# Transposing the 32 left-over columns of x before or after the split into high and low parts

## The chip, the cores and the metric

The kernel runs on one core of a Trainium2 chip. The metric is the device time of one execution in microseconds (us); the time before is the median of three runs.

## The reference

```python
x = A_x                                   # 1 x 2048 x 576
xn = _layernorm(x, axis=-1)
return x + _A_ref(xn, A_w_r, A_w_i) + _B_ref(xn, B_w_gate, B_w_up, B_w_down)

def _A_ref(x, w_r, w_i):                  # spectral filter
    X = jnp.fft.rfft2(x, axes=(-2, -1)) * (w_r + 1j * w_i)
    return jnp.fft.irfft2(X, s=(S, D), axes=(-2, -1))

def _B_ref(x, w_gate, w_up, w_down):      # gated linear unit, 576 -> 4608 -> 576
    h = _sigmoid(x @ w_gate) * (x @ w_up)
    return h @ w_down
```

All inputs are float32. S = 2048 rows, D = 576 columns, F = 4608 hidden columns.

## The kernel before

Every large product runs on TensorE in F32R, a reduced form of float32. To keep the accuracy, each operand is split into a high part (rounded to F32R by a ScalarE copy) and a low part (VectorE subtracts the high part from the original), and three products are added: high x high, low x high, high x low.

The gated unit is the main load. The 2048 rows are handled as two pairs of chunks of 512 rows (`p` = 0, 1). In each pair the 576 columns are halved (288 each), and most products use a seven-product scheme on 2 x 2 blocks: A11, A12, A21, A22 and the sums S1 to S4 of such blocks. For each of the 36 hidden tiles, `unit` (or `plain` for the first two tiles) runs products (`prod`, L648) of 512-wide matmuls; the down projection (`down`, L755) and later the "seven" rounds (L846) and the spectral stages (`phase1b`, `phase2`, `phase3`) are threaded between them by generators that are advanced once in each product (`beside`, `turn`).

The products need x with columns on the partitions, so each block of the normalized x is transposed on TensorE. A block is 128 rows x 288 columns: two tiles of 128 columns and 32 left-over columns (`REM`). The tile `X` holds, for each block and each of its 512 rows, five slices: the high parts of the two 128-column tiles (slices 0 and 1), the left-over slice (2), and the two low parts (3 and 4). The left-over slice has 96 used partitions (`KR` = 3 x 32): the 32 columns' high part twice and their low part once; the weights stand against it as high, low, high, so that one matmul does all three products. `STEPS` puts it last of the seven matmuls of a product.

The functions around the change, with the names that the views show:

- `prep` normalizes a row tile into `xa` (L409) and then splits its left-over columns into `rma`: `rem_hi` writes the high part twice with one ScalarE copy (L391), `rem_lo` the low part with one VectorE subtraction (L396). `sums` forms the sums of blocks (L421 to L424) and splits the left-over columns of the results into `rma` and `rm34` (shown as `rm`).
- `fill` brings one block for two row tiles into `X`. It takes a pair of PSUM banks (`px`, from a pool of two pairs that the down projection and the spectral stages use too), does four transposes of 128 x 128 against the F32 identity `idf` (L438) and two of the split 96 columns against the F32R identity `idr` (L439), copies the results into `X` on ScalarE (L442 for the wide tiles, L443 for the left-over slice), and subtracts on VectorE for the low parts (L444).

There are 32 fills: in each of the two pairs, two for each of A11, A12, A21, A22 and S1 to S4. The first four come at the start of the kernel, ahead of the first product; twelve more fall within the first part of the first pair, and sixteen at the change to the second pair, all among products.

At the start a list of matmuls on the identity (`todo`, L904) keeps TensorE occupied; some use all 128 rows, some the halves `H0` and `H1`. Four more (L922) stand between the first fills.

A scheduler places each instruction on its engine at build time, by estimated times; `placed` and `keep_in_program_order` hold some of them to the written order.

Of the kernel before, what the change touches and what calls it, by code (L numbers as in the profile page):

```python
# [10 lines left out]
F32R = mybir.dt.float32r  # L11
I32 = mybir.dt.int32
AF = mybir.ActivationFunctionType
OP = mybir.AluOpType
PSUM = bass.MemoryType.PSUM

P = 128
# [9 lines left out]
TPC = CW // P  # L27
PAIRS = S // (2 * CW)
TPP = 2 * TPC
KT = 2  # L30
REM = HD - KT * P
# [6 lines left out]
KR = 3 * REM  # L38
# [94 lines left out]
def spectral_glu_kernel(ctx: ExitStack, tc: tile.TileContext, x, w_r, w_i, w_gate, w_up, w_down, out):  # L133
    nc = tc.nc
    con = {k: nc.inline_tensor(v, name=f"c_{k}").ap() for k, v in _constants().items()}

    def f32(ap):
        return ap.bitcast(F32)
# [6 lines left out]
    def pair(name):  # L145
        return ps.tile([P, 2, 512], F32, tag="pp", name=name, bufs=2)

    fix = ctx.enter_context(tc.tile_pool(name="fix", bufs=1))
    idf = fix.tile([P, P], F32, name="idf")
    idr = fix.tile([P, P], F32R, name="idr")  # L150
# [49 lines left out]
    R = {}  # L200
# [23 lines left out]
    def placed(ins):  # L224
        if late_input[0]:
            tc.keep_in_program_order(ins)
# [121 lines left out]
    def moments(src, t, pool):  # L348
        st = pool.tile([P, 2, 6], F32, tag="st", name=f"st{t}", bufs=2)
        for i in range(2):  # L350
            placed(nc.vector.bn_stats(st[:, i, :], src[:, i * HD:(i + 1) * HD]))
        nc.vector.bn_aggr(mv[:, t, :], st.rearrange("p a b -> p (a b)"))

    def scales(t0, n, pool, table):
        ts = slice(t0, t0 + n)
        rs = pool.tile([P, 4, n], F32, tag="rs", name=f"rs{t0}", bufs=2)
        ve, r0, w0, w1 = (rs[:, i] for i in range(4))
        nc.vector.tensor_scalar(ve, mv[:, ts, 1], EPS, None, op0=OP.add)
        if table:
            nc.scalar.activation(w0, ve, AF.Sqrt)  # L360
            nc.vector.reciprocal(r0, w0)
            steps = 1
        else:

            nc.vector.tensor_scalar(w1.bitcast(I32), ve.bitcast(I32), 1, None, op0=OP.logical_shift_right)
            nc.vector.tensor_scalar(r0.bitcast(I32), w1.bitcast(I32), -1.0, float(0x5F3759DF), op0=OP.mult, op1=OP.add)
            steps = 3
        nc.vector.tensor_scalar(ve, ve, -0.5, None, op0=OP.mult)
        for k in range(steps):
            nc.vector.tensor_tensor(w0, r0, r0, op=OP.mult)  # L370
            nc.vector.tensor_tensor(w0, w0, ve, op=OP.mult)
            o = rstd[:, ts] if k == steps - 1 else r0
            nc.vector.scalar_tensor_tensor(o, w0, 1.5, r0, op0=OP.add, op1=OP.mult)
        nc.vector.scalar_tensor_tensor(nmr[:, ts], mv[:, ts, 0], -1.0, rstd[:, ts], op0=OP.mult, op1=OP.mult)
# [5 lines left out]

    XS, XR, RM = {}, {}, {}

    def new_xs(p, m):
        XS[m] = R["pool"].tile([P, 5, HD], F32, tag="xa", name=f"xa{p}_{m}", bufs=TPC)

    def rem_hi(p, m, i, tag, bufs):
        rem = XS[m][:, i:i + 2, KT * P:]
        rm = R["pool"].tile([P, 2, 3, REM], F32R, tag=tag, name=f"{tag}{p}_{m}_{i}", bufs=bufs)  # L390
        nc.scalar.activation(rm[:, :, :2], rem.unsqueeze(2).to_broadcast([P, 2, 2, REM]), AF.Copy)  # L391
        RM[m, i] = rm

    def rem_lo(m, i):
        rm = RM[m, i]
        placed(nc.vector.tensor_tensor(rm[:, :, 2], XS[m][:, i:i + 2, KT * P:], f32(rm[:, :, 0]), op=OP.subtract))  # L396
        for k in range(2):
            XR[m, i + k] = rm[:, k].rearrange("p a b -> p (a b)")

    def rem_parts(p, m, i, tag, bufs):  # L400
        rem_hi(p, m, i, tag, bufs)
        rem_lo(m, i)

    def prep_hi(p, m, c):

        t = p * TPP + c * TPC + m
        b = XS[m][:, 2 * c:2 * c + 2]
        src = b if p else acc[t].rearrange("p (a d) -> p a d", a=2)
        nc.scalar.activation(b, src, AF.Identity, bias=nmr[:, t:t + 1], scale=rstd[:, t:t + 1])  # L409
        rem_hi(p, m, 2 * c, "rma", 2)  # L410

    def prep_lo(m, c):
        rem_lo(m, 2 * c)

    def prep(p, m, c):
        prep_hi(p, m, c)
        prep_lo(m, c)

    def sums(p, m):
        A11, A12, A21, A22, S1 = (XS[m][:, i] for i in range(5))  # L420
        nc.vector.tensor_tensor(S1, A21, A22, op=OP.add)  # L421
        nc.vector.tensor_tensor(A21, A11, A21, op=OP.subtract)
        nc.vector.tensor_tensor(A22, S1, A11, op=OP.subtract)
        nc.vector.tensor_tensor(A12, A12, A22, op=OP.subtract)  # L424
        rem_parts(p, m, 3, "rma", 2)
        rem_parts(p, m, 1, "rm34", TPC)

    XP = {"A11": 0, "A12": 1, "A21": 2, "A22": 3, "S4": 1, "S3": 2, "S2": 3, "S1": 4}

    def fill(p, k, mm):  # L430

        i, j0 = XA[k], XP[k]
        cols = slice(2 * mm * P, (2 * mm + 2) * P)
        pt = pair(f"px{p}_{k}_{mm}")
        for j in range(2):
            m = 2 * mm + j
            for q in range(KT):
                nc.tensor.transpose(pt[:, 0, (2 * q + j) * P:(2 * q + j + 1) * P], XS[m][:, j0, q * P:(q + 1) * P], idf)  # L438
            nc.tensor.transpose(pt[:KR, 1, j * P:(j + 1) * P].bitcast(F32R), XR[m, j0], idr)  # L439
        v = pt[:, 0].rearrange("p (q s) -> p q s", q=KT)  # L440
        o = X[:, i, :, cols]
        nc.scalar.activation(o[:, :KT], v, AF.Copy)  # L442
        nc.scalar.activation(o[:KR, KT], pt[:KR, 1, :2 * P], AF.Copy)  # L443
        nc.vector.tensor_tensor(o[:, KT + 1:], v, f32(o[:, :KT]), op=OP.subtract)  # L444

    def new_acc(p, m):
        t = p * TPP + m
        acc[t] = AC[:, m]
        load_x(acc[t], t)
# [460 lines left out]
        moments(acc[m], m, R["pool"])  # L910
    scales(0, 2, R["pool"], True)
    for m in (0, 1):
        prep_hi(0, m, 0)
    for m in (2, 3):
        moments(acc[m], m, R["pool"])
    for m in (0, 1):
        prep_lo(m, 0)
    scales(2, 2, R["pool"], True)
    for k in ("A11", "A12"):
        fill(0, k, 0)  # L920
    for n in range(4):
        tc.keep_in_program_order(nc.tensor.matmul(b0, idr, eye, start=False, stop=True, skip_group_check=True))  # L922
    for m in (2, 3):
        prep(0, m, 0)
    next(mk)
    next(mk)
    for k in ("A11", "A12"):
        fill(0, k, 1)
# [17 lines left out]
    def blocks(p, c):  # L946
        for mm in range(2):
            for m in (2 * mm, 2 * mm + 1):
                prep(p, m, c)
            for k in (1, 2):  # L950
                fill(p, f"A{c + 1}{k}", mm)
            yield
# [20 lines left out]
    def factors(p):  # L973

        for mm in range(2):
            for m in (2 * mm, 2 * mm + 1):
                sums(p, m)
                yield
            for k in ("S1", "S2"):
                fill(p, k, mm)  # L980
                yield
            if mm == 0:
                sides.append(late(p))
# [162 lines left out]
```

## Time and profile before

| | before |
|---|---|
| median of 3 runs | 1441.58 us (1441.42 to 1442.97) |
| profiled execution, span from first to last instruction | 1439.6 us |
| profiled execution, time of its own beside the span | not given by the page |
| TensorE matmuls busy | 1425.9 us (99%) |
| TensorE weight loads busy | 1254.3 us (87%) |
| VectorE busy | 1093.5 us (76%) |
| ScalarE busy | 652.3 us (45%) |
| mean granted TensorE clock | 0.996 |

In the profile PE is TensorE's matmuls, PEld its weight loads, DVE VectorE, ACT ScalarE, SP the queue that issues most transfers. A row such as `128*96 128x128` gives the rows and columns of the stationary operand and then the shape of the moving one. The busy time of a matmul runs from its start to its modelled end, and matmuls overlap; the chain of work that ended last shows instead how far each one moved the end.

### The profile page before, as it was taken

The page shows a single profiled execution, that of the slowest core. Times are in us where ns is not written, and L with a number is a line of the kernel's source. Part 1 is how long each engine was busy: PE and PEld are TensorE (multiplying, and loading weights), DVE is VectorE, ACT ScalarE, POOL GpSimd, SP SyncE. Part 2 cuts the span into 40 slices and gives each one's busy share as a digit, 9 for nine tenths or more (in the row PEclk, how much of TensorE's full clock was granted, in tenths as well). Part 3 has the DMA queues.
Part 4 walks back from the last instruction along what each step waited for, and adds up shares of the span by engine and source line. Part 5 has one row for each costly group of instructions (what it writes and reads, how often), then busy time and mean ns, then how long its engine had stood idle before and what let it go on. Part 6 is the DMA issues. An engine that isn't in the chain of part 4 may idle for free.

```text
span 1439.6 us, 21954 instructions
## 1 busy us (share of the span) xinstructions
PE 1425.9 (99%) x8073; PEld 1254.3 (87%) x8073; DVE 1093.5 (76%) x1798; ACT 652.3 (45%) x1122; POOL 4.8 (0%) x21
## 2 busy tenths in 40 slices
PE   8999999999999999999999999999999999999998
PEld 5888888888888888888888888888888889899997
DVE  6988788888888888756366787767888877766784
ACT  5644444444444444444345444444555534443432
POOL 0000000000000000000000000000000000000000
PEclk8999999999999999999999999999999999999999
DMA  6588788787777778664667767668998887776642
GB/s 209 207 277 294 263 295 285 254 274 258 263 261 255 262 254 277 230 231 167 226 210 203 212 197 214 196 198 275 271 275 272 267 276 246 228 224 198 204 126 83
DMA packets 184747, 338.86 MB, mean 235 GB/s; under 512 B 15808, under 2 KB 108480, under 8 KB 179776
## 3 DMA queue, kind: packets, MB, share of 16 engines
q1 hardware_dynamic: 183712, 336.15, 72.2%
q8 instruction: 64, 1.05, 0.3%
q10 hardware_dynamic: 928, 1.31, 0.3%
q14 instruction: 43, 0.35, 0.1%
HBM read 201.28 MB, written 136.12 MB: 234 GB/s over the span
## 4 chain that ended last, share of the span: by engine, by line
PE 94%; DVE 2%; DMA 1%; SPq 1%; ACT 1%; issue 1%; DVEq 0%; ACTq 0%
PE pB L648 23%; PE po L755 18%; PE pE L648 16%; PE pA L648 15%; PE ps L846 12%; PE pd L491 2%; PE pe L605 2%; PE pc L549 1%; PE py L576 1%; PE pa L503 1%; PE pb L532 1%; DMA raw<-in_B_w_up 1%; PE pf L475 1%; PE pz L588 1%; SPq L218 0%
## 5 line engine op out<-in xcount | busy, mean ns | idle before, releaser
L648 PE MATMUL pB<-X,w 128*128 128x512 f32 x1484 | 383.0, 395 | 1.9 <-ACT w L231 1.5
L648 PEld LDWEIGHTS pB<-X,w 128*128 128x128 f32 x1484 | 267.8, 188 | 51.8 <-ACT w L231 1.9
L648 PE MATMUL pE<-X,w 128*128 128x512 f32 x1064 | 272.5, 392 | 0.2 <-DVE y L713 0.2
L648 PE MATMUL pA<-X,w 128*128 128x512 f32 x1008 | 259.4, 395 | 0.3 <-DVE X L444 0.2
L648 PEld LDWEIGHTS pE<-X,w 128*128 128x128 f32 x1064 | 192.7, 188 | 34.6 <-DVE y L713 0.7
L648 PEld LDWEIGHTS pA<-X,w 128*128 128x128 f32 x1008 | 184.5, 190 | 33.9 <-DVE X L444 0.7
L755 PE MATMUL po<-wd,hh 128*128 128x288 f32 x1216 | 210.9, 295 | 0.0
L846 PE MATMUL ps<-wf,hs 128*128 128x288 f32 x1260 | 206.0, 296 | 0.3 <-issue 0.3
L846 PEld LDWEIGHTS ps<-wf,hs 128*128 128x128 f32 x1260 | 189.3, 188 | 19.4 <-DVE qs L856 1.9
L755 PEld LDWEIGHTS po<-wd,hh 128*128 128x128 f32 x1216 | 184.4, 188 | 11.2
L759 DVE TENSOR_TENSOR acc<-acc,po 128x576 f32<-128x576 f32 x168 | 126.0, 750 | 77.9 <-PE po L755 76.8
L231 ACT ACTIVATE w<-raw 128x768 fp32r<-128x768 f32 (+1 forms) x106 | 100.8, 952 | 115.6 <-PE pE L648 47.5
L755 PE MATMUL po<-wd,hl 128*128 128x288 f32 x608 | 128.9, 293 | 0.0
L856 DVE TENSOR_TENSOR qs<-qs,ps 128x576 f32<-128x576 f32 x112 | 84.1, 751 | 28.6 <-PE ps L846 27.9
L755 PEld LDWEIGHTS po<-wd,hl 128*128 128x128 f32 x608 | 98.7, 189 | 0.0
L733 DVE TENSOR_TENSOR y<-y,g 128x1024 f32<-128x1024 f32 x67 | 82.0, 1223 | 4.4 <-DVE y L732 0.5
L233 DVE TENSOR_TENSOR w<-raw,w 128x512 fp32r<-128x512 f32 (+1 forms) x106 | 82.0, 773 | 4.3 <-ACT w L231 3.3
L856 DVE TENSOR_TENSOR acc<-acc,ps 128x576 f32<-128x576 f32 x90 | 67.5, 750 | 22.9 <-PE ps L846 22.5
L716 ACT ACTIVATE g<-pB 128x512 f32<-128x512 f32 x68 | 40.7, 598 | 93.6 <-PE pB L648 93.5
L782 ACT ACTIVATE hs<-y 128x512 fp32r<-128x512 f32 x105 | 64.5, 628 | 34.3 <-DVE y L820 10.3
L732 DVE TENSOR_TENSOR y<-v,pE 128x512 f32<-128x512 f32 x67 | 45.9, 686 | 39.4 <-PE pE L648 39.3
L713 DVE TENSOR_TENSOR y<-v,pE 128x512 f32<-128x512 f32 x68 | 46.7, 687 | 33.7 <-ACT v L712 33.0
(166 smaller groups left out, 1678.8 us busy)
## 6 DMA issues: line engine op xcount, KB each, us to landing
w<-wsp SPq DMA_DIRECT2D x246, 320.0 KB
wsp<-w SPq DMA_DIRECT2D x34, 2240.0 KB
wdsp<-wd SPq DMA_DIRECT2D x36, 576.0 KB
wf<-tsp SPq DMA_DIRECT2D x60, 288.0 KB
wf<-wdsp SPq DMA_DIRECT2D x45, 288.0 KB
std<-in_B_w_down SPq DMA_DIRECT2D x36, 288.0 KB
raw<-in_B_w_gate SPq DMA_DIRECT2D x72, 128.0 KB
raw<-in_B_w_up SPq DMA_DIRECT2D x72, 128.0 KB
```

Of the source, the lines that this page charges most:

```text
L231: placed(nc.scalar.activation(o[:, :, :3, :], src, AF.Copy))
L233: placed(nc.vector.tensor_tensor(o[:, :, 3:, :], src[:, :, :KT, :], f32(o[:, :, :KT, :]), op=OP.subtract))
L648: nc.tensor.matmul(bank, w[:, sw, :], X[:, x, sx, :], start=start and j == 0, stop=stop and j == len(STEPS) - 1, skip_group_check=skip)
L713: nc.vector.tensor_tensor(y[:, 1], v[:, 1], bank["E"], op=OP.add)
L716: nc.scalar.activation(g[:, 1], bank["B"], AF.Sigmoid)
L732: nc.vector.tensor_tensor(y[:, 0], v[:, 0], bank["E"], op=OP.add)
L733: nc.vector.tensor_tensor(y, y, g, op=OP.mult)
L755: nc.tensor.matmul(pd[:, b, :HD], h[i], w[k][b], start=g == 0 and n == 0, stop=g == G - 1 and n == 2)
L759: nc.vector.tensor_tensor(a, a, pd[:, :, :HD], op=OP.add)
L782: nc.scalar.activation(hs[:, 0], src, AF.Copy)
L846: nc.tensor.matmul(pd[:, i, :HD], h[:, a, m], w[:, b], start=q == 0, stop=q == 2)
L856: nc.vector.tensor_tensor(o, o, pd[:, :, :HD], op=OP.add)
```

## The change

The left-over columns are no longer split before the transpose. `rem_hi`, `rem_lo`, `rem_parts`, `prep_hi` and `prep_lo` go, and with them the tiles `rma` and `rm34`. `fill` transposes the 32 columns as they are, in F32 against `idf`, into 32 partitions of PSUM. Behind the transpose ScalarE copies them twice (to partitions 0 to 31 and 32 to 63 of the left-over slice), and VectorE subtracts the first copy from the transposed columns and writes the low part to partitions 64 to 95.

```diff
-    def rem_hi(p, m, i, tag, bufs):
-        rem = XS[m][:, i:i + 2, KT * P:]
-        rm = R["pool"].tile([P, 2, 3, REM], F32R, tag=tag, name=f"{tag}{p}_{m}_{i}", bufs=bufs)
-        nc.scalar.activation(rm[:, :, :2], rem.unsqueeze(2).to_broadcast([P, 2, 2, REM]), AF.Copy)
-        RM[m, i] = rm
-
-    def rem_lo(m, i):
-        rm = RM[m, i]
-        placed(nc.vector.tensor_tensor(rm[:, :, 2], XS[m][:, i:i + 2, KT * P:], f32(rm[:, :, 0]), op=OP.subtract))
-        for k in range(2):
-            XR[m, i + k] = rm[:, k].rearrange("p a b -> p (a b)")
...
-    def prep_hi(p, m, c):
+    def prep(p, m, c):
...
         nc.scalar.activation(b, src, AF.Identity, bias=nmr[:, t:t + 1], scale=rstd[:, t:t + 1])
-        rem_hi(p, m, 2 * c, "rma", 2)
...
     def sums(p, m):
...
         nc.vector.tensor_tensor(A12, A12, A22, op=OP.subtract)
-        rem_parts(p, m, 3, "rma", 2)
-        rem_parts(p, m, 1, "rm34", TPC)
...
     def fill(p, k, mm):
...
-            nc.tensor.transpose(pt[:KR, 1, j * P:(j + 1) * P].bitcast(F32R), XR[m, j0], idr)
+            nc.tensor.transpose(pt[:REM, 1, j * P:(j + 1) * P], XS[m][:, j0, KT * P:], idf)
         v = pt[:, 0].rearrange("p (q s) -> p q s", q=KT)
         o = X[:, i, :, cols]
         nc.scalar.activation(o[:, :KT], v, AF.Copy)
-        nc.scalar.activation(o[:KR, KT], pt[:KR, 1, :2 * P], AF.Copy)
+        rest = pt[:REM, 1, :2 * P]
+        for n in range(2):
+            nc.scalar.activation(o[n * REM:(n + 1) * REM, KT], rest, AF.Copy)
         nc.vector.tensor_tensor(o[:, KT + 1:], v, f32(o[:, :KT]), op=OP.subtract)
+        nc.vector.tensor_tensor(o[2 * REM:KR, KT], rest, f32(o[:REM, KT]), op=OP.subtract)
...
     for m in (0, 1):
-        prep_hi(0, m, 0)
+        prep(0, m, 0)
     for m in (2, 3):
         moments(acc[m], m, R["pool"])
-    for m in (0, 1):
-        prep_lo(m, 0)
     scales(2, 2, R["pool"], True)
```

More of the change, by code (lines that the diff above doesn't have):

```diff
@@ L379, in norm @@
             nc.vector.tensor_scalar(o, a, mv[:, t, 0:1], rstd[:, t:t + 1], op0=OP.subtract, op1=OP.mult))
-    XS, XR, RM = {}, {}, {}
+    XS = {}
     def new_xs(p, m):
         XS[m] = R["pool"].tile([P, 5, HD], F32, tag="xa", name=f"xa{p}_{m}", bufs=TPC)
-    def rem_hi(p, m, i, tag, bufs):
-        rem = XS[m][:, i:i + 2, KT * P:]
-        rm = R["pool"].tile([P, 2, 3, REM], F32R, tag=tag, name=f"{tag}{p}_{m}_{i}", bufs=bufs)
-        nc.scalar.activation(rm[:, :, :2], rem.unsqueeze(2).to_broadcast([P, 2, 2, REM]), AF.Copy)
-        RM[m, i] = rm
-    def rem_lo(m, i):
-        rm = RM[m, i]
-        placed(nc.vector.tensor_tensor(rm[:, :, 2], XS[m][:, i:i + 2, KT * P:], f32(rm[:, :, 0]), op=OP.subtract))
-        for k in range(2):
-            XR[m, i + k] = rm[:, k].rearrange("p a b -> p (a b)")
-    def rem_parts(p, m, i, tag, bufs):
-        rem_hi(p, m, i, tag, bufs)
-        rem_lo(m, i)
-    def prep_hi(p, m, c):
+    def prep(p, m, c):
         t = p * TPP + c * TPC + m
@@ L409, in prep_hi @@
         nc.scalar.activation(b, src, AF.Identity, bias=nmr[:, t:t + 1], scale=rstd[:, t:t + 1])
-        rem_hi(p, m, 2 * c, "rma", 2)
[L412 to L417, printed above, removed]
     def sums(p, m):
```

## The prediction

> **What bounds the kernel now.** I read the profile's head and its chain first, to see which engine sets the end.
>
> ```profile
> span 1439.6 us, 21954 instructions
> ...
> PE 1425.9 (99%) x8073; PEld 1254.3 (87%) x8073; DVE 1093.5 (76%) x1798; ACT 652.3 (45%) x1122; POOL 4.8 (0%) x21
> ...
> PE 94%; DVE 2%; DMA 1%; SPq 1%; ACT 1%; issue 1%; DVEq 0%; ACTq 0%
> ```
>
> TensorE is busy for 99% of the span and carries 94% of the chain that ended last. So microseconds taken from VectorE (76%) or ScalarE (45%) count only where TensorE waits for them, and a nanosecond added to a TensorE instruction counts in full nearly everywhere. The second view is the list of what TensorE's matmuls waited for; these are its rows that touch the transposes and the start:
>
> ```profile
> PE px_A L438 <- ACT xa L409: 1.5, 2, 1.1
> PE pB L648 <- ACT w L231: 1.5, 1, 1.5
> PE px_A L439 <- DVE rma L396: 0.6, 1, 0.6
> PE px_S L438 <- DVE X L444: 0.5, 1, 0.5
> ```
>
> The columns are total us, times, longest. The split that the change removes (rma, L391 and L396) held TensorE up once, for 0.6 us. That is all the change can win from a wait. The third view is the chain through one fill (two row tiles, six transposes), which shows what each transpose costs on the engine that sets the end:
>
> ```profile
> 43.49 0.22 PE px_S L438 x2
> 43.70 0.06 PE px_S L439
> 43.76 0.22 PE px_S L438 x2
> 43.98 0.06 PE px_S L439
> ```
>
> The chain counts the step from one end to the next, so pipelining is already taken out. Two F32 transposes of 128 columns take 0.22 us, 0.11 each. The F32R transpose of the 96 already split columns takes 0.06. No step is lost between the two kinds, though they alternate.
>
> **The change part by part.** How many instructions of each kind there are, and how long one takes, is in the line views:
>
> ```profile
> L439 PE MATMUL px_A<-idr,rma x32: 222/304/455, 10.6 to 659.7; 128*96 128x128 f32 x32
> L439 PE MATMUL px_S<-idr,rma x16: 303/304/308, 43.5 to 693.3; 128*96 128x128 f32 x16
> L439 PE MATMUL px_S<-idr,rm x16: 302/304/308, 55.5 to 705.3; 128*96 128x128 f32 x16
> L391 ACT ACTIVATE rma<-xa x24: 293/310/329, 10.0 to 686.8; 128x128 fp32r<-128x128 f32 x24
> L391 ACT ACTIVATE rm<-xa x8: 309/312/320, 35.7 to 667.6; 128x128 fp32r<-128x128 f32 x8
> L396 DVE TENSOR_TENSOR rma<-xa,rma x24: 215/219/227, 10.3 to 687.6; 128x64 fp32r<-128x64 f32 x24
> L396 DVE TENSOR_TENSOR rm<-xa,rm x8: 218/218/221, 39.9 to 668.2; 128x64 fp32r<-128x64 f32 x8
> L443 ACT ACTIVATE X<-px_A x16: 366/372/392, 11.7 to 660.8; 96x256 fp32r<-96x256 f32 x16
> L443 ACT ACTIVATE X<-px_S x16: 366/371/392, 44.6 to 706.3; 96x256 fp32r<-96x256 f32 x16
> L235 DVE TENSOR_TENSOR w<-raw,w x106: 414/416/555, 16.2 to 627.5; 32x256 fp32r<-32x256 f32 x72, 32x384 fp32r<-32x384 f32 x34
> ```
>
> ScalarE loses 32 splits of 0.31 us (9.9 us) and gains 32 more copies of a 256-wide remainder. It had one such copy a fill, 0.37 us on 96 partitions; with 32 partitions I keep 0.37, since the width sets it: 11.8 us. Net +1.9 us on an engine that is 45% busy. VectorE loses 32 x 0.22 = 7.0 us and gains 32 subtractions of 32x256, which L235 shows at 0.416: 13.3 us, net +6.3 us on an engine that is 76% busy. Neither sum is on TensorE's path by itself. The order within a fill does change, and one late fill shows who stands behind it:
>
> ```profile
> 46.29 0.60 ACT L442 ACTIVATE X<-px_S 128x512 fp32r<-128x512 f32 x1
> 46.79 0.37 ACT L443 ACTIVATE X<-px_S 96x256 fp32r<-96x256 f32 x1
> 47.05 0.68 ACT L290 ACTIVATE wd<-std 128x576 fp32r<-128x576 f32 x1
> 47.19 0.69 DVE L444 TENSOR_TENSOR X<-px_S,X 128x512 fp32r<-128x512 f32 x1 [0.41 <-ACT X L443]
> 47.80 0.75 DVE L292 TENSOR_TENSOR wd<-std,wd 128x576 fp32r<-128x576 f32 x1
> ```
>
> L444 starts behind the last ScalarE copy (L443), not behind L442 alone. With two copies there it starts one copy step (46.79 to 47.05, 0.26 us) later. The new subtraction waits for those copies too, and adds 0.42 behind L444. Queued behind it are the split of w_down on VectorE (L292) and on ScalarE (L290); nobody on TensorE needs those soon. The new subtraction's own result is read only by the last of a product's seven matmuls, which hides it. What is exposed is the PSUM pair, held up to 0.26 + 0.42 = 0.7 us longer (two pairs serve all), and the low part that a product's second matmul reads. Today that is the 0.5 us wait for L444 above. I put nothing on them in the steady part, because TensorE itself will be later by more than that in each fill (below), and 2 us as their bound. If TensorE is not later, a few tenths of them show.
>
> Now the 64 transposes themselves. They change from F32R with 96 columns to F32 with 32 columns. The trace has no transpose so narrow. By the rows above one costs between 0.06 (the F32R step) and 0.11 (the F32 step). The data type changes and the streamed identity stays 128 wide, so I take the F32 row, 0.11: +0.05 each. The upper bound is 0.22, a further doubling.
>
> The larger term is whether TensorE can go between a 32-column and a 128-column transpose without stopping. The nearest rows are the warm-up matmuls at the start, which alternate between the whole array and 64-row halves of it (weight loads, then a stretch of ordinary products, then the granted clock):
>
> ```profile
> 7.09 0.93 PEld L904 LDWEIGHTS b<-idr 64*128 64x128 f32 x6 [0.65 <-issue]
> 8.40 0.30 PEld L904 LDWEIGHTS b<-idr 128*128 128x128 f32 x2 [0.38 <-issue]
> 9.06 0.19 PEld L904 LDWEIGHTS b<-idr 64*128 64x128 f32 x2 [0.36 <-issue]
> 9.48 0.19 PEld L904 LDWEIGHTS b<-idr 128*128 128x128 f32 x1 [0.24 <-issue]
> 38.70 3.20 PE pA L648 x14
> 8.04:14.86 6.82, 4.98 (x30) 2.96 (x26) 5.19 (x21) 5.92 (x14) 0.00 (x0) 1.00 0.66 186
> 14.86:21.69 6.83, 6.58 (x19) 4.87 (x20) 5.62 (x13) 2.92 (x6) 0.00 (x0) 0.50 0.65 166
> ```
>
> All are 512 wide. A product's matmul of that width takes 3.20/14 = 0.229 us. From 8.40 to 9.06, at a granted clock of 1.00, two whole-array matmuls took 0.66 instead of 0.46: 0.20 more. From 9.06 to 9.48 one pair of halves, loaded together within 0.19 us, took 0.42 instead of 0.23: 0.19 more. The loads sit idle before each change and for no other instruction ("issue"). I read this as the array being set up anew and emptied first, 0.2 us at each change of shape. In the Trainium skill, "TensorEngine Tiling (Array Packing)", Key Properties, changing the tiling mode drains TensorE; these rows agree for row tiles, and none shows a column tile. The same page's Restrictions say that column tiling excludes the FP32 transpose mode, which no row here tests.
>
> A 32-column transpose stands alone among 128-column ones (T T R T T R, then products), so each of the 64 brings two changes: 2 x 0.20 + 0.05 = 0.45 us. The first 8 lie ahead of TensorE's wait at 27.3 us:
>
> ```profile
> L439 PE MATMUL px_A<-idr,rma x8: 222/306/455, 10.6 to 15.9; 128*96 128x128 f32 x8
> 27.31 3.01 PE L648 MATMUL pB<-X,w 128*128 128x512 f32 x7 [1.50 <-ACT w L231]
> ```
>
> They cost 8 x 0.45 = 3.6 us, against 1.1 us (the longest wait for L409) and 1.5 us (for w, L231) in which TensorE waits anyway, so 1.0 is left. The other 56 lie where TensorE hardly waits: 56 x 0.45 = 25.2. The sum is +26.2 us. The 0.6 us wait for rma lies among the first 8, whose rest is not sharper than that; I leave it out. The forecast is 1441.6 + 26.2 = 1467.8 us (span 1439.6 + 26.2 = 1465.8; the page gives no other time of the profiled execution, and the 2.0 us between its span and the median stay as they are). If a change of shape costs half of that, it is 56 x 0.25 = +14 (1455.6); with a transpose of 0.22 it is 64 x 0.56 = +36 (1477.6).
>
> **The rivals.** *No stop, only the dearer data type.* The columns are simply fewer and the array keeps its shape. For it: the 96- and 128-column transposes already alternate without loss. Against it: those two keep most of the columns, while the 64-row halves, which do not keep most of the rows, were set apart at 7.09 to 9.48. It gives 56 x 0.05 = 2.8 us, plus 0.2 to 0.5 us of late L444, so 1444.8 (1442 to 1446).
>
> *Nothing on TensorE.* A 32-column F32 transpose costs the 0.06 of today. Then only the 0.6 us wait goes and some 0.3 us of late L444 comes: 1441.3, no difference. For it speaks only that the trace has no F32 row under 128 columns.
>
> *Not slower: the load sets the step.* If the 0.11 of an F32 transpose were the load of its 128 columns, 32 columns would take 0.11/4 = 0.03. Then 64 x 0.03 = 1.9 us go, with the rma wait 2.5, and 3 to 4 us if an earlier start also shortens the stretch at half clock (14.86 to 21.69, the row with 0.50 above): 1437.5 to 1439.7, say 1438.6. It decides as soon as the step of a narrow transpose falls below 0.06. Against it: the loads of neighbours start closer together than that step.
>
> ```profile
> 43.33 0.14 PEld L438 LDWEIGHTS px_S<-idf,xa 128*128 128x128 f32 x1
> ...
> 43.54 0.20 PEld L438 LDWEIGHTS px_S<-idf,xa 128*128 128x128 f32 x2
> ```
>
> Two loads span 0.20 and one lasts 0.14, so the second began 0.06 after the first, and a load of 128 columns does not hold the engine for 0.11. "TensorE: Matmul & The Clock Gate" in the Trainium skill, section on LDWEIGHTS, has the load time grow with the columns (columns/1.2 ns); by it 96 columns would take 80 ns, and the step measured here is 60.
>
> **How the numbers follow.** The forecast's case has a chance of 0.64, the dearer type alone 0.20, nothing on TensorE 0.08, the load 0.08. What a measurement of this kernel can tell from no change is about 0.2%, 2.9 us. The forecast's case is slower by more than that throughout; of the second case I count 0.13 beyond it and 0.07 within; the third is within; the fourth is 0.05 faster and 0.03 within. So slower 0.77, same 0.18, faster 0.05. The forecast's own range is 1455.6 to 1477.6. To leave out no more than 2 in 10 the range must reach over the second case and the edge of the third: 1441 to 1477.
>
> **What would show it.** If the forecast is right, the weight loads of L438 and of the products that follow a 32-column transpose sit idle for 0.1 to 0.4 us with "issue" as releaser, and a fill in the chain takes about 1.5 us in place of 0.56, for 32 fills. TensorE's instruction count stays 8073, ScalarE's stays 1122 and VectorE's 1798, as 32 go and 32 come on each. If the second case holds, the chain shows 0.11 steps throughout and no idle loads. A 32-column step of 0.06 or less, or a span below 1446, would make the forecast wrong. A TensorE wait for L444 or its new neighbour of over 2 us in sum would show that I covered that edit too cheaply.

## The result, and the profile after

| | before | after |
|---|---|---|
| median | 1441.4 us (1441.34 to 1442.97, 6 runs) | 1445.93 us (1445.05 to 1446.56, 6 runs) |
| profiled execution: own time, span | not given, 1439.6 us | 1445.05 us, 1442.9 us |
| ratio to before | | 1.003 (95%: 1.0019 to 1.0042) |

The change costs 4.5 us, 0.3%. The direction was the forecast one, the size was not: 26.2 us had been expected, and the time lies in the range's low end, at the place of the second case.

The head of the page after, with its chain:

```profile
span 1442.9 us, 21979 instructions
...
PE 1425.4 (99%) x8073; PEld 1252.8 (87%) x8073; DVE 1103.5 (76%) x1798; ACT 658.3 (46%) x1122; POOL 4.8 (0%) x21
...
PE 95%; DVE 2%; ACT 1%; issue 1%; DMA 0%; SPq 0%; DVEq 0%; ACTq 0%
```

The counts are as predicted (8073, 1798, 1122). The chain through the fill that the prediction showed at 43.49 us:

```profile
43.27 0.22 PE px_S L412 x2
43.49 0.11 PE px_S L413
43.59 0.22 PE px_S L412 x2
43.81 0.11 PE px_S L413
43.92 1.61 PE pE L625 x7
```

L412 is the old L438, L413 the 32-column transpose, L625 the old L648. The narrow transpose takes 0.11 us a step, like a wide one. A fill takes 0.66 us and not 1.5: nothing stops. The last row here is to be read beside the row behind the same fill in the kernel before:

```profile
44.04 1.66 PE pE L648 x7
```

Seven product matmuls took 1.66 us behind an F32R transpose and take 1.61 behind an F32 one. So of the 2 x 0.05 us that the fill became dearer, 0.05 comes back in the product behind it. From 43.49 to 45.70 before and from 43.27 to 45.53 after, fill and seven matmuls take 2.21 and 2.26 us.

The instructions of the new lines behind the transpose (L419 the copies, L421 the new subtraction; the half of each that works on `px_S`):

```profile
L419 ACT ACTIVATE X<-px_S x32: 355/366/375, 44.5 to 710.5; 32x256 fp32r<-32x256 f32 x32
L421 DVE TENSOR_TENSOR X<-px_S,X x16: 415/416/418, 45.9 to 711.6; 32x256 fp32r<-32x256 f32 x16
```

Both durations were sized right (0.366 and 0.416 us). The busy time of the page rises by more than they add up to: by 10.0 us on VectorE and 6.0 on ScalarE, where the prediction had 6.3 and 1.9. It counts the time in which two instructions overlap once, and the new ones overlap their neighbours less (shown at e2 for ScalarE).

What TensorE's matmuls waited for after the change (total us, times, longest):

```profile
PE pB L625 <- ACT w L231: 2.6, 1, 2.6
...
PE pE L625 <- DVE X L420: 1.4, 1, 1.4
PE pA L625 <- DVE X L420: 0.9, 1, 0.9
PE px_S L412 <- DVE X L421: 0.4, 2, 0.2
...
PE po L732 <- DVE X L421: 0.2, 1, 0.2
```

L420 is the old L444, the wide subtraction. TensorE now waits 2.3 us for it and 0.6 us for the new L421, against 0.7 us for L444 before. That is 2.9 us, over the 2 us that the prediction named as the sign of having covered this edit too cheaply. The wait of 0.9 us stands at 17.6 us, ahead of the wait for the weights, so 1.4 us of the 2.3 count. The largest of these waits, on ScalarE, TensorE and VectorE:

```profile
53.23 0.35 ACT L419 ACTIVATE X<-px_S 32x256 fp32r<-32x256 f32 x1
53.67 0.85 ACT L231 ACTIVATE w<-raw 128x768 fp32r<-128x768 f32 x1
54.54 0.37 ACT L419 ACTIVATE X<-px_S 32x256 fp32r<-32x256 f32 x1
54.69 0.69 DVE L652 TENSOR_TENSOR y<-g,pE 128x512 f32<-128x512 f32 x1
55.30 0.69 DVE L233 TENSOR_TENSOR w<-raw,w 128x512 fp32r<-128x512 f32 x1
56.00 0.41 DVE L235 TENSOR_TENSOR w<-raw,w 32x256 fp32r<-32x256 f32 x1
56.44 0.69 DVE L420 TENSOR_TENSOR X<-px_S,X 128x512 fp32r<-128x512 f32 x1
57.19 0.74 PE L625 MATMUL pE<-X,w 128*128 128x512 f32 x2 [1.41 <-DVE X L420]
```

The second copy stands behind a weight split on ScalarE (L231), and the wide subtraction behind three other instructions on VectorE; so the low part is there at 57.13 us, and the product that reads it has stood since its first matmul. In the kernel before, the same subtraction ran at 54.22 us. The chain of the kernel before, in the same place:

```profile
50.39 0.23 DVE rma L396
...
54.22 0.69 DVE X L444
54.91 0.60 DVE w L233
```

So VectorE led here before the change already: from 49.8 to beyond 65 us that chain holds nothing but VectorE's instructions and the gaps between them, the split of the left-over columns among them. What is added to VectorE here counts, although TensorE hardly waits.

To see where the time went in all, I matched the 3556 product matmuls (L648 and L625) of the two traces one to one, and took the difference of their starts (after less before, us; the place is the time in the kernel before):

| place, us | 27.3 | 55.9 | 76.7 | 652.6 | 728.8 |
|---|---|---|---|---|---|
| after | -0.6 | -0.5 | +2.0 | +1.8 | +3.5 |

The whole change comes in two stretches of fills: +2.5 us between 56 and 77 us, and +1.7 us between 653 and 729 us. In the second, the chain of the kernel before holds TensorE alone. After the change it leaves TensorE from 704.3 to 708.8 us, for ScalarE's copies of two fills in a row (L416 the wide one, L419 the two narrow ones), the two subtractions, and a transpose that waits for the PSUM pair:

```profile
705.59 0.25 ACT X L419
...
705.86 0.37 ACT X L419
...
706.25 0.60 ACT X L416
706.85 0.25 ACT X L419
...
707.12 0.38 ACT X L419
...
707.52 0.69 DVE X L420
...
708.23 0.43 DVE X L421
...
708.79 0.41 PE px_S L412 x2
```

The start costs nothing in this execution, which needs one remark: its granted clock differs by execution. A stretch of the profile after:

```profile
14.86:21.69 6.83, 5.67 (x28) 4.25 (x27) 5.66 (x12) 4.00 (x9) 0.00 (x0) 1.00 0.69 187
```

The profile after had the full clock (1.00) from 14.86 to 21.69 us, where the profile before had half. TensorE then waits longer for the weights (2.6 us for L231, before 1.5), and at 27.3 us the two are within 0.6 us of each other.

### The profile page after: what moved, and what is told of

Read it like the earlier page. It is cut to its first block, busy times and chain, and to the rows that moved or that the text cites. A ratio compares the mean times of both kernels' runs of the same rounds, so it can differ in the third digit from the quotient of the medians.

```text
span 1442.9 us, 21979 instructions
## 1 busy us (share of the span) xinstructions
PE 1425.4 (99%) x8073; PEld 1252.8 (87%) x8073; DVE 1103.5 (76%) x1798; ACT 658.3 (46%) x1122; POOL 4.8 (0%) x21
## 4 chain that ended last, share of the span: by engine, by line
PE 95%; DVE 2%; ACT 1%; issue 1%; DMA 0%; SPq 0%; DVEq 0%; ACTq 0%
PE pB L625 23%; PE po L732 18%; PE pE L625 16%; PE pA L625 16%; PE ps L823 12%; PE pd L468 2%; PE pe L582 2%; PE pc L526 1%; PE py L553 1%; PE pa L480 1%; PE pb L509 1%; PE pf L452 1%; PE pz L565 0%; PE b L881 0%; PE px_A L412 0%
## 5 line engine op out<-in xcount | busy, mean ns | idle before, releaser
L625 PE MATMUL pB<-X,w 128*128 128x512 f32 x1484 | 383.6, 395 | 3.1 <-ACT w L231 2.6
L625 PEld LDWEIGHTS pB<-X,w 128*128 128x128 f32 x1484 | 268.1, 189 | 53.6 <-ACT w L231 3.1
L625 PE MATMUL pE<-X,w 128*128 128x512 f32 x1064 | 273.2, 393 | 1.4 <-DVE X L420 1.4
L625 PE MATMUL pA<-X,w 128*128 128x512 f32 x1008 | 257.8, 393 | 1.2 <-DVE X L420 0.9
L625 PEld LDWEIGHTS pE<-X,w 128*128 128x128 f32 x1064 | 192.8, 188 | 35.7 <-DVE X L420 1.8
L625 PEld LDWEIGHTS pA<-X,w 128*128 128x128 f32 x1008 | 182.9, 188 | 33.9 <-DVE X L420 1.2
L231 ACT ACTIVATE w<-raw 128x768 fp32r<-128x768 f32 (+1 forms) x106 | 100.8, 952 | 107.6 <-PE pE L625 46.8
L833 DVE TENSOR_TENSOR acc<-acc,ps 128x576 f32<-128x576 f32 x90 | 67.6, 751 | 22.4 <-PE ps L823 22.0
```

Source lines behind the costliest of these rows:

```text
L231: placed(nc.scalar.activation(o[:, :, :3, :], src, AF.Copy))
L625: nc.tensor.matmul(bank, w[:, sw, :], X[:, x, sx, :], start=start and j == 0, stop=stop and j == len(STEPS) - 1, skip_group_check=skip)
L833: nc.vector.tensor_tensor(o, o, pd[:, :, :HD], op=OP.add)
```

## The experiments

The theory after seeing this: columns never stop the array; the F32 step costs about 1.4 us (28 fills of 0.05); the rest, some 3 us, is the new ScalarE and VectorE work behind the transposes. The rivals: the narrow shape costs TensorE something that the chain hides; the F32 transposes carry it all; it is the place of the wide subtraction alone.

**What a change of shape costs (e4).** Rows of matmuls behind the kernel before. `wide` is a 512-wide F32R matmul and `turned` a transpose; `full` is the whole identity, `thin` 32 columns of it, `half` 64 rows; `FR32` is two full F32 transposes and a thin one. Cut, with the definitions left out:

```diff
...
+    for nm, fs in (("sa", [lambda o: wide(o, *full)] * 12),
+                   ("sb", [lambda o: wide(o, *full), lambda o: wide(o, *thin)] * 6),
+                   ("sc", [lambda o: wide(o, *full), lambda o: wide(o, *half)] * 6),
+                   ("sd", [lambda o: wide(o, *thin)] * 12),
+                   ("se", [lambda o: turned(o, *full)] * 12),
+                   ("sf", [lambda o: turned(o, *thin)] * 12),
+                   ("sg", FR32 * 5),
+                   ("sh", [lambda o: turned(o, none, KR, F32R)] * 12),
+                   ("si", [lambda o: turned(o, none, REM, F32R)] * 12)):
...
```

> The kernel before with rows of matmuls on the identity added behind its last product, whose results nobody reads: 512-wide F32R matmuls with 128 columns, alternating with 32 columns (sb), alternating with 64 rows (sc), 32 columns alone (sd), F32 transposes of 128 (se), of 32 (sf), two of 128 and one of 32 in turn (sg), F32R transposes of 96 (sh) and of 32 columns (si). Theory (columns never stop the array, rows do): sb steps of 0.23 us like sa, sc steps near 0.42, se, sf and sg all 0.11, sh and si 0.06. Rival (a change of columns stops the array too, and only the transposes escape it): sb near 0.42 like sc.

By tile, with the durations in ns, the first and last start in us, and the forms:

```profile
L1129 PE MATMUL sa<-X,idr x12: 388/389/395, 1435.1 to 1437.6; 128*128 128x512 f32 x12
L1129 PE MATMUL sb<-X,idr x12: 391/393/503, 1438.1 to 1440.7; 128*128 128x512 f32 x6, 128*32 128x512 f32 x6
L1129 PE MATMUL sc<-X,idr x12: 491/502/794, 1441.2 to 1446.4; 128*128 128x512 f32 x6, 64*128 64x512 f32 x6
L1134 PE MATMUL se<-idf x12: 272/273/328, 1452.4 to 1453.7; 128*128 128x128 f32 x12
L1134 PE MATMUL sf<-idf x12: 272/273/286, 1454.0 to 1455.2; 128*32 128x128 f32 x12
L1134 PE MATMUL sg<-idf x15: 272/273/329, 1455.5 to 1457.1; 128*128 128x128 f32 x10, 128*32 128x128 f32 x5
L1134 PE MATMUL sh<-idr x12: 230/234/268, 1457.5 to 1458.3; 128*96 128x128 f32 x12
L1134 PE MATMUL si<-idr x12: 222/222/236, 1458.6 to 1459.2; 128*32 128x128 f32 x12
```

Twelve matmuls have eleven steps between the first start and the last: 2.5/11 = 0.23 us for the whole array (sa), 2.6/11 = 0.24 when every other one has 32 columns (sb; its first step took 0.34 us, the others 0.23). With 64 rows in every other one (sc) it is over 0.4; at the full clock its weight loads show it one by one, and sit idle before each:

```profile
1441.59 0.18 PEld L1129 LDWEIGHTS sc<-X,idr 64*128 64x128 f32 x1 [0.25 <-issue]
1442.02 0.19 PEld L1129 LDWEIGHTS sc<-X,idr 128*128 128x128 f32 x1 [0.25 <-issue]
```

That is 0.43 us a step, 0.20 more than sa. (The row sd ran at half clock and says nothing.) The F32 transposes step by 0.11 us wide, narrow and mixed (se 1.3/11 = 0.12, sf 1.2/11 = 0.11, sg 1.6/14 = 0.11), the F32R ones by 0.07 (sh, 0.8/11) and 0.06 (si, from its first start at 1458.56 to its last at 1459.23 us). So a change from 128 to 64 rows stops the array and a change from 128 to 32 columns does not, transposes or not. The theory holds, and the rival that only transposes escape falls.

**Width (e2).** The unsplit transpose with 96 columns:

```diff
-            nc.tensor.transpose(pt[:REM, 1, j * P:(j + 1) * P], XS[m][:, j0, KT * P:], idf)
+            nc.tensor.transpose(pt[:KR, 1, j * P:(j + 1) * P], XS[m][:, j0, HD - KR:], idf)
...
-        rest = pt[:REM, 1, :2 * P]
+        rest = pt[2 * REM:KR, 1, :2 * P]
```

> The changed kernel, but the unsplit transpose takes 96 columns (the 32 left-over ones and the 64 ahead of them) and the copies read the last 32 partitions of the result. Everything else is as in the change. Theory (32 columns cost TensorE the same 0.11 step as 128, the array is not stopped for them): same as the changed kernel, 1445 to 1446.6. Rival (a narrow transpose still costs something beyond its step): 64 x that less; with 0.02 us each 1.3 us less.

It took 1447.2 us (ratio to before 1.0042, 1.0028 to 1.0055): not faster, and outside the expected range on the slow side by 0.6 us. As something else made it slower, the time alone can't tell whether a narrow transpose costs something beyond its step. The chain can: the 96-column transposes step by 0.11 us here too (695.42 to 695.53 us), and e4 has 0.11 for 32 columns alone and mixed. The chain shows one difference, at the place of the two copies that began the chain rows of the change above (705.59 and 705.86 us):

```profile
707.40 0.38 ACT X L419
...
707.79 0.38 ACT X L419
```

Here the first copy moves the end by 0.38 us, there by 0.25. The starts and ends of ScalarE's instructions in the traces show a pattern. In the change, the first copy reads partitions 0 to 31 and writes 0 to 31; it starts 0.10 us before the wide copy ahead of it ends (median of 30). The second one writes 32 to 63; it starts 0.01 us behind the first (31 of 31), and what follows starts 0.02 us behind it. Here both copies move the columns, from 64 to 95 down to 0 to 31 and to 32 to 63, and neither overlaps its neighbours (0.01 us behind, 0.02 us behind). With the unmoved copy alone (e7, below) the overlap is there on both sides, 0.10 and 0.09 us, as it was for L443 in the kernel before (0.10 and 0.11). So a copy to other partitions than it reads cost ScalarE the overlap with both neighbours in these traces. The second copy of the change therefore took a step of 0.38 us and held the next instruction up besides, where the prediction had 0.26. No kernel changed the partitions alone; that these steps carry the 1.3 us by which e2 is slower than the change is argued and not shown.

**The data type alone (e1).** The kernel before with F32 for its split transposes:

```diff
-            nc.tensor.transpose(pt[:KR, 1, j * P:(j + 1) * P].bitcast(F32R), XR[m, j0], idr)
+            nc.tensor.transpose(pt[:KR, 1, j * P:(j + 1) * P], f32(XR[m, j0]), idf)
```

> The kernel before, split ahead of the transpose as it was, but its 64 transposes of the 96 split columns run in F32 against the F32 identity. Theory (the data type sets the step): each goes from 0.06 to 0.11 us, 56 on the path, so +2.8 us with the order unchanged, at most 64 x 0.05 = +3.2; 1444.2 to 1444.6. Rival (the narrow shape and the new work behind the transpose are what costs, the type nothing): 1441.4, no difference.

Measured: 1442.3 us, ratio 1.0008 (0.9999 to 1.0017), that is +1.0 us, below the +2.8 of the theory and clear of neither no change nor of 1.4. Its chain shows the same exchange as the changed kernel's, 0.11 for the transpose and 1.61 behind it:

```profile
43.85 0.11 PE px_S L439
43.96 1.61 PE pE L648 x7
```

So the type costs about half of what its step says, 28 x 0.05 = 1.4 us by the chain and 1.0 by the time.

**The new work behind the transpose (e5, e6, e7).** From the changed kernel, the second copy and the new subtraction are left out, both or one of them; the partitions that they would fill are set to zero once at the start, which is not shown. The three kernels in one cut, with remarks:

```diff
...
-        for n in range(2):
+        for n in range(1):                     # e5, e7: one copy
             nc.scalar.activation(o[n * REM:(n + 1) * REM, KT], rest, AF.Copy)
         nc.vector.tensor_tensor(o[:, KT + 1:], v, f32(o[:, :KT]), op=OP.subtract)
-        nc.vector.tensor_tensor(o[2 * REM:KR, KT], rest, f32(o[:REM, KT]), op=OP.subtract)   # e5, e6: no low part
```

> The changed kernel without the work behind the transpose that is new: the second copy of the 32 columns and their low part are left out (those partitions hold zeros), so the left-over columns count at reduced accuracy. Theory (of the change's 4.5 us, 1 to 1.6 are the F32 step, the rest is the new ScalarE and VectorE work between a fill's transposes and its low parts): 1442.3 to 1443.0. Rival (the narrow F32 transposes carry the 4.5 us themselves): 1445 to 1446.6.

> The changed kernel with both copies but without the VectorE subtraction for the low part of the 32 columns (zeros in its place). Theory A (the wide subtraction's wait for the second copy is what costs, so the copies carry it): near the changed kernel, 1445. Theory B (VectorE's extra 0.42 us a fill carries it, by holding the PSUM pair and by pushing the next subtraction back): near the kernel without both, 1442.3 to 1443.0.

> The changed kernel with the subtraction but only one copy of the 32 columns (zeros where the second would be). Theory A (the second copy carries the cost): 1442.3 to 1443.0. Theory B (the subtraction carries it): near the changed kernel, 1445.

| kernel | median, us | ratio to before (95%) | more than before, us |
|---|---|---|---|
| e5, neither | 1442.86 | 1.0012 (1.0003 to 1.0020) | +1.7 |
| e6, two copies, no subtraction | 1444.88 | 1.0025 (1.0016 to 1.0034) | +3.7 |
| e7, one copy, subtraction | 1444.68 | 1.0022 (1.0013 to 1.0030) | +3.5 |
| the change (its own runs) | 1445.93 | 1.0030 (1.0019 to 1.0042) | +4.5 |

With the narrow F32 transposes and none of the new work the kernel costs 1.7 us, as the theory has it. Each of the two additions brings about 1.9 us by itself (2.0 and 1.8), and both together 2.8 (the change was timed apart from the three). Neither theory A nor B holds: the work of either engine is enough.

**The same work on the kernel before (e9).**

```diff
         nc.scalar.activation(o[:KR, KT], pt[:KR, 1, :2 * P], AF.Copy)
+        nc.scalar.activation(pt[:REM, 1, 2 * P:], pt[:REM, 1, :2 * P], AF.Copy)
         nc.vector.tensor_tensor(o[:, KT + 1:], v, f32(o[:, :KT]), op=OP.subtract)
+        nc.vector.tensor_tensor(pt[2 * REM:KR, 1, 2 * P:], pt[:REM, 1, :2 * P], f32(o[:REM, KT]), op=OP.subtract)
```

> The kernel before, transposes and split as they were, with the change's new work added to each fill for nothing: one more 32x256 ScalarE copy between the copy of the left-over slice and the wide subtraction, and one more 32x256 VectorE subtraction behind it, both into an unused part of the same PSUM bank. Theory (what is left of the change's cost beside the F32 step is this work behind the transpose, whatever the transpose is): +2 to +3.3 us, 1443.2 to 1444.5. Rival (the work is hidden, and the cost comes from the F32 transposes or from the order in which the changed kernel's instructions were placed): 1441.0 to 1441.8.

Measured: 1445.6 us, ratio 1.0032 (1.0019 to 1.0044), +4.4 us. The work costs without any change of the transposes, so the rival that the F32 transposes carry the cost falls. It is 1 us more than expected, which fits that here the split ahead of the transposes is still done as well; that was not tried apart. Three of its waits:

```profile
PE pA L650 <- DVE X L445: 2.0, 2, 1.0
PE px_A L438 <- ACT px_A L444: 1.6, 1, 1.6
PE px_A L438 <- DVE px_A L446: 1.3, 1, 1.3
```

L444 and L446 are the two added lines, L445 the wide subtraction behind one of them. The 1.6 us and one of the two waits for L445 (0.9 us) lie ahead of 28 us; at 27.3 us this kernel is level with the one before (table below).

**The place of the wide subtraction (e3).**

```diff
+        nc.vector.tensor_tensor(o[:, KT + 1:], v, f32(o[:, :KT]), op=OP.subtract)
         rest = pt[:REM, 1, :2 * P]
         for n in range(2):
             nc.scalar.activation(o[n * REM:(n + 1) * REM, KT], rest, AF.Copy)
-        nc.vector.tensor_tensor(o[:, KT + 1:], v, f32(o[:, :KT]), op=OP.subtract)
```

> The changed kernel with one line moved: in a fill the subtraction for the wide low parts is written ahead of the two copies of the left-over columns, not behind them. Theory (what the change costs beyond 0.05 us a transpose is this subtraction waiting behind two copies, 1.4 and 0.9 us of TensorE's waits in its profile): those two waits go, 1443.5 to 1444.2. Rival (the rest is the clock and the order of the start): 1445 to 1446.6, no difference from the changed kernel.

Measured: 1446.01 us, ratio 1.0034 (1.0022 to 1.0047): no gain. Of the waits for the wide subtraction 0.2 us is left, and these came:

```profile
PE px_S L412 <- DVE X L421: 1.5, 2, 0.8
PE po L732 <- DVE X L421: 1.5, 1, 1.5
```

They stand for a PSUM pair that the new subtraction still reads. The theory that the place of one line costs the time fell. That suggested the pair itself.

**Freeing the pair early (e10).**

```diff
-        rest = pt[:REM, 1, :2 * P]
-        for n in range(2):
-            nc.scalar.activation(o[n * REM:(n + 1) * REM, KT], rest, AF.Copy)
+        rest = R["pool"].tile([P, 2 * P], F32, tag="rest", name=f"rest{p}_{k}_{mm}", bufs=2)[:REM]
+        nc.scalar.activation(rest, pt[:REM, 1, :2 * P], AF.Copy)
         nc.vector.tensor_tensor(o[:, KT + 1:], v, f32(o[:, :KT]), op=OP.subtract)
+        for n in range(2):
+            nc.scalar.activation(o[n * REM:(n + 1) * REM, KT], rest, AF.Copy)
```

> The changed kernel, but ScalarE first copies the 32 transposed columns once to SBUF in full precision; the two high copies and the low part are then made from there, behind the wide subtraction. ScalarE has one 32x256 copy more in each fill, VectorE the same work. Theory (the PSUM pair held longer and the wide subtraction behind two copies is what costs): the pair is free after one copy as before, so only the F32 step of 0.7 to 1.4 us and a few tenths are left, 1442.3 to 1443.5. Rival (the engines' added time itself costs, wherever it stands): 1445.5 or more.

Measured: 1447.68 us, ratio 1.0041 (1.0027 to 1.0054). The theory of the pair fell too: there is no gain. But it does not show the rival either. The kernel has a copy more on ScalarE, so two things changed at once. And the 1.7 us by which its median is above the change's are not from the fills among products, as far as the traces show: two of its five runs, at 1446.1 us, are as fast as the change, and the profiled execution (1447.68 us) is behind that of the change by 2.7 us at 55.9 us already, and by 2.3 us at 728.8. In the two stretches of fills it loses about as much as the change (2.1 and 2.1 us against 2.5 and 1.7 in the table below).

Starts of the product matmuls against the kernel before, in the profiled executions, as in the table above:

| place, us | 27.3 | 55.9 | 76.7 | 652.6 | 728.8 |
|---|---|---|---|---|---|
| e1, F32 on the kernel before | 0.0 | 0.0 | +0.3 | 0.0 | +0.8 |
| e5, the change without the new work | -0.3 | +0.4 | +1.4 | +0.9 | +1.5 |
| e6, with two copies | -0.4 | -0.4 | +2.2 | +1.6 | +3.2 |
| e7, with the subtraction | -0.4 | -0.4 | +1.7 | +1.3 | +2.8 |
| the change | -0.6 | -0.5 | +2.0 | +1.8 | +3.5 |
| e2, 96 columns | -0.2 | 0.0 | +2.9 | +3.0 | +5.6 |
| e3, wide subtraction first | +0.4 | -0.6 | +1.5 | +2.8 | +4.5 |
| e9, the work on the kernel before | 0.0 | +1.2 | +3.0 | +1.2 | +4.0 |
| e10, one copy more | +0.9 | +2.2 | +4.2 | +3.7 | +5.8 |

The additions act in the same two stretches in each of them. e3 and e9 also differ between the two, +1.3 and -1.8 us, and e9 and e10 ahead of them.

How busy the two engines are in these stretches, in the kernel before (the stretch and its length, then the busy us of PE, PEld, DVE, ACT and POOL):

```profile
27.50:65.00 37.50, 36.55 (x191) 29.48 (x191) 33.52 (x70) 29.30 (x61) 0.00 (x0) 0.95 0.52 182
652.00:712.00 60.00, 60.00 (x361) 52.77 (x360) 31.94 (x63) 23.29 (x55) 0.13 (x2) 1.00 0.60 206
```

In the first stretch VectorE is busy for 89% and ScalarE for 78%: there is little room. In the second it is 53% and 39%, and there the shares don't explain the cost. There it is a short burst, the one of the chain at 704.3 to 708.8 us. In e5 the chain holds TensorE alone in this stretch; in e6 it leaves TensorE from 704.0 to 707.9 us, for ScalarE. In e7 it does not leave TensorE for more than 0.1 us, so how the subtraction alone costs its part there stays open.

**A version that might beat both (e8).** The short F32R transpose between two F32 ones, in the kernel before:

```diff
             for q in range(KT):
                 nc.tensor.transpose(pt[:, 0, (2 * q + j) * P:(2 * q + j + 1) * P], XS[m][:, j0, q * P:(q + 1) * P], idf)
-            nc.tensor.transpose(pt[:KR, 1, j * P:(j + 1) * P].bitcast(F32R), XR[m, j0], idr)
+                if q == 0:
+                    nc.tensor.transpose(pt[:KR, 1, j * P:(j + 1) * P].bitcast(F32R), XR[m, j0], idr)
```

> The kernel before, with its F32R transpose of the 96 split columns written between the two 128-column transposes of a row tile instead of behind them. Theory (a product's first matmul behind an F32R transpose takes 0.05 us more, as its chain rows show 1.66 against 1.61 for seven, because its 128-column load does not fit under the short transpose; a 128-column F32 transpose there hides it): 28 to 32 times 0.05, so -1.4 to -1.6 us, 1439.8. Rival (the 0.05 moves to the F32 transpose behind it, or the earlier need of the split is waited for): 1441.3 or more.

Measured: 1440.05 us, ratio 0.9992 (0.9983 to 1.0001): 1.1 us less, not clear of no change. Its chain shows the product behind a fill (after the F32 transpose L438) at 1.63 in place of 1.66:

```profile
689.22 0.11 PE px_S L438
689.33 1.63 PE pE L649 x7
```

But its profiled execution gained only 0.2 us between 653 and 729 us, where 16 x 0.05 = 0.8 was expected, and had 2.1 us of gain by 56 us already, from the start. So the reason given for it is not what the time shows.

## Why the prediction was wrong, point by point

- **The step that failed** is the larger term, "0.2 us at each change of shape", carried over from 64-row halves to 32 columns. The price was read right: e4 has 0.43 us a step in sc against 0.23 in sa. It does not hold for columns: sb steps like sa, and the chain after the change has 0.11 throughout. 56 x 0.40 = 22.4 us of the 25.2 were not there, and neither was the 1.0 us that was left of the first 8. In the Trainium skill, "TensorEngine Tiling (Array Packing)", Key Properties, a change of the tiling mode drains TensorE. The runs here agree for halves of 64 rows. For 32 columns they show no stop, although the built program gives these matmuls a tile size of 128 x 32; whether the array changes its mode for them no trace shows. By its Restrictions column tiling excludes the FP32 transpose mode; no run shows whether that mode was off here, and the narrow F32 transposes step like the wide ones (0.11 us).
- **The F32 step** of 0.11 for the narrow transpose was right, and its cost of 0.05 each was not: half of it comes back in the product's first matmuls (1.61 for 1.66). The term of 2.8 us is 1.0 to 1.4 us (e1, the chain), or 1.7 with the narrow form (e5); the intervals of e1 and e5 overlap.
- **The work behind the transpose** was sized right in each instruction (0.366 and 0.416 us) and covered wrongly. The cover that I named was TensorE's own delay; I wrote that without it "a few tenths" would show. With the delay gone it costs 2.8 us (the change against e5). I had the two places, the PSUM pair and the low part, and the bound of 2 us on them. Two things were missed. I took it that work on VectorE and ScalarE counts only where the list of TensorE's waits shows it; but in the kernel before the chain was VectorE's from 49.8 to beyond 65 us, so in these fills the sums on VectorE were on the path. And I sized the second copy as a step of 0.26 us like the first; it took 0.38 us, without overlap on either side.
- **The second case** (no stop, 1444.8) was right that nothing stops, and 1.1 us low by two errors of opposite sign: the step too dear by 1.1 (e5) to 1.4 us (the chain), the new work too cheap by about 2.5. That its figure lies so close is in part luck.
- **The start** was put at 1.0 us and cost nothing: at 27.3 us the profile after is 0.6 us ahead. That TensorE's wait for the first weights covers what the first fills lose was right; the loss was smaller than the 3.6 us put on them.

Open: how much of the 2.8 us is time on ScalarE and VectorE as such, and how much the order in which the scheduler puts their instructions when the estimates change. In the change, e5, e6 and e7 that order is nearly the one before: without the lines of the fill and of the split, all 7881 instructions of TensorE, at least 1022 of the 1026 of ScalarE and 1709 of the 1734 of VectorE stand in the same order in the traces. In e3, e9 and e10 more moved (973 to 975 on ScalarE, 1584 to 1623 on VectorE keep their order), so these three show less.

## What to carry to other kernels

A price measured for one kind of change in shape is not the price of another: before it is multiplied by 64, it is worth asking which dimension the row shows. Where an edit puts work on engines that do not bound the kernel, read the chain in the stretch in which the edit sits, and not the shares of the whole span: two small instructions a fill cost 2.8 us, more than the dearer transposes did (1.0 to 1.7), and the chain of the kernel before was already on VectorE in the first of the two stretches. A shorter TensorE instruction need not pay in full: the F32R transpose was 0.05 us shorter, and the seven matmuls behind it took 0.05 us more. Why they do is not shown; e8, which was built on one reason, did not gain where that reason said.

## What the hardware showed that I had not expected

- Alternating 128 and 32 columns costs nothing (0.24 us a step for 512-wide matmuls against 0.23, 0.11 for F32 transposes), while alternating 128 and 64 rows adds 0.20 us at every change.
- An F32 transpose steps by 0.11 us whether it has 32, 96 (e1) or 128 columns; an F32R one of 96 columns steps by 0.06 between F32 ones, and the seven matmuls behind it take 1.66 us where they take 1.61 behind an F32 one.
- A ScalarE copy of 32 x 256 that writes the partitions it reads started 0.10 us before its predecessor ended; one that writes other partitions started 0.01 us behind it, and what followed 0.02 us behind that (the change, e2, e7).
